# A fused attention and two-layer MLP kernel: third part of the values' product moved and widened, first loads on a second queue, schedule chosen anew

## The chip, the cores and the metric

The kernel runs on one core of one Trainium2 chip. The time is the device time of one execution in microseconds (us); the median of three runs of the kernel before is 1149.66 us (1148.32 to 1153.46). A profiled execution of the same kernel took 1149.11 us, and its trace spans 1147.1 us from the first to the last instruction.

## The reference

Attention over 4 batches and 8 heads, 576 tokens, head size 64, in which only scores within `tau` of a row's maximum count. Its output, as a 2304 x 512 matrix, goes through two MLP blocks with the weights' inner size 2048: the first with a squared ReLU, the second with a leaky ReLU.

```python
scores = scale * np.matmul(q, k.transpose(0, 1, 3, 2))
thresh = np.max(scores, axis=-1, keepdims=True) - tau
scores = np.where(scores >= thresh, scores, -1000000000.0)
attn = np.exp(scores - np.max(scores, axis=-1, keepdims=True))
attn = attn / (np.sum(attn, axis=-1, keepdims=True) + 1e-09)
attn_out = np.matmul(attn, v)
x = attn_out.transpose(0, 2, 1, 3).reshape(2304, 512)
h = x @ moe_w_in;  x = (np.maximum(h, 0) ** 2) @ moe_w_out
h = x @ moe2_w_in; x = np.maximum(0.01 * h, h) @ moe2_w_out
```

The weights arrive as 64-bit floats.

## The kernel before

**Attention.** Heads are taken in 16 pairs (`order`, four to a batch), and each pair in nine steps (`steps`): a step is 128 query rows of one head against all 576 keys, or, once in a pair, the last 64 rows of both heads. A step does its scores on PE (line 497), a row maximum on DVE (L507), the exponential on ACT (L508), threshold and sum on DVE (L512), and the normalization. In the first four pairs (`nav=4`) the normalized weights are turned on PE (L531) and multiplied with the values in fp32 (L597). From the fifth pair on they are split into a high and a low 16-bit part in one row `P16` of 1216 columns (576 high, the first 64 of them again, 576 low), turned by a DMA transpose (L559) and multiplied with the values by `av` (L593).

**The values' product (`values`).** For a chunk of 256 or 320 queries there are nine 128-row pieces of turned weights: four high, one that holds 64 high rows and 64 low rows, and four low. The values are split in a part `hi` that lies as 128 columns in `VA`, and a third part `low` of 64 columns in `VB`. A chunk is 15 matmuls: five with `hi` (128x128), four with `low` against the high pieces (64 columns, alternately in the lower and the upper half of the output), two with `low` against the mixed piece (its first 64 rows alone, half of the queries each), and four more with `hi` (128x128). There are 12 pairs with four chunks each, 48 chunks. ACT (L605, L607), POOL or DVE (L610) add the two halves of the output, and a DMA stores them in `x1d`.

**MLP.** `w_block` loads a block of raw weights (128 x 512 64-bit floats, 512 KB), turns them into fp32 in three DVE instructions (L341, L343, L345) and one on ACT (L340), and splits them into two fp32r parts (L285 or L287, then a subtraction on POOL or DVE, L296/L298). The raw blocks share a ring of three buffers (`wraw`). While attention runs, `ffn` takes 256 tokens at a time through 12 of the 16 blocks of the first layer (L641 and L665). After it the rest of the first layer and the second layer run in blocks of 512 tokens (L774 and L820), and the second layer's blocks of weights are prepared meanwhile.

**What sets the order.** Nothing is written out by hand: every operation is handed to `Plan.op` with its possible engines, a cost and a priority (an attention step number plus a constant of `CFG`). `Plan.order` simulates the engines with these costs, gives each operation to an engine (the multipliers `price` weigh the engines against each other), and issues all in the order of the simulated starts. So a changed constant can move operations in time and between engines anywhere. All loads and stores go through `dma` and are issued by SP; two small loads (`tau`, `eye`) are issued by ACT.

Of the kernel before, what the change touches and what calls it, by code (L numbers as in the profile page):

```python
# [18 lines left out]
P = 128  # L19
# [7 lines left out]
           {'V': 3.0, 'A': 0.99, 'G': 0.8},  # L27
           {'V': 2.4, 'A': 1.42, 'G': 1.25},
           {'V': 2.43, 'A': 1.06, 'G': 0.97},
           {'V': 3.0, 'A': 2.4, 'G': 1.02}],  # L30
    lead1=-2.0, xsg0=[0, 1, 2], lbm=8, lb=[[0, 2, 4, 6], [0], [2, 5], [1, 3, 5, 6]], xsm=4, xsg=[0, 3], dq=1.15,
    xu=False, pqk=-2.283, pd1=-0.75, pex=-1.0, pd2=0.3, ph=2.017, pl=1.4, hu=True, bg=2.008, lead=2.5, w0=22.0,
    wstep=2.3, fend=1.0, tol=0.2, hor=-0.015, xlead=5.801, nb=3, eb=3, pb=3, ptb=3, kvb=3, nat=(0, 1, 2, 3, 4, 5),
    nav=4, vb=2, tmb=1, gb=2, xb=1, w2step=2.0, wo=0.316, wrb=3, r1b=1, xrb=1,
# [211 lines left out]
def tile_kernel(ctx: ExitStack, tc: tile.TileContext, qT, kT, vv, w1, w2, tau, eye, out):  # L246
# [57 lines left out]
    def dma(o, i, r, w, prio, nbytes, **k):  # L304
        return op(("S", 0.06, lambda: nc.sync.dma_start(out=o(), in_=i())), r, w, prio, dma=move(nbytes), **k)
# [15 lines left out]
    def w_block(pool, src, f, tag, prio, after=()):  # L321
# [3 lines left out]
        for g, io in enumerate("io"):  # L325
# [4 lines left out]
            c = slice(g * W, (g + 1) * W)  # L330
            if wide:
# [7 lines left out]
                dma(lambda raw=raw: raw.get()[:, 0:2 * W].bitcast(I32), lambda c=c: src[f][:, c].bitcast(I32), [], [raw], pr - 1, P * W * 8, after=after)  # L339
# [69 lines left out]
    def prep(n):  # L409
# [9 lines left out]
        if n in CFG["nat"]:  # L419
# [6 lines left out]
            for h in range(2):  # L426
                dma(lambda h=h: qs(h)[h * D:(h + 1) * D], lambda h=h: qT[b, h0 + h], [], [Q], at(0), D * S * 4)
# [474 lines left out]
```

## Time and profile before

| | |
|---|---|
| runs, median (lowest to highest) | 1149.66 us (1148.32 to 1153.46) |
| profiled execution, its span | 1149.11 us, 1147.1 us |
| busy: PE, DVE, POOL, ACT | 94%, 60%, 55%, 47% of the span |
| mean granted TensorE clock | 0.990 of full speed |
| DMA | 121.82 MB, mean 106 GB/s |

An average over the span hides three stages. Up to about 125 us only attention runs; then attention and the MLP share PE until about 560 us; from there PE works almost without a gap to the end. The views by stretch show which engine is full in each, and the lists of waits show who is late.

### The profile page before, as it was taken

How to read it: one execution, taken by the hardware profiler on the slowest of the kernel's cores; microseconds unless marked ns; L12 is line 12 of the kernel's file. 1: busy time of each engine (PE TensorE's matmuls, PEld its weight loads, DVE VectorE, ACT ScalarE, POOL GpSimd, SP SyncE). 2: the span in 40 equal slices, each digit the busy share in tenths (PEclk: the TensorE clock that was granted, in tenths of full speed). 3: DMA queues.
4: the chain of work that ended last, by engine and by line, in shares of the span. 5: the costliest groups of instructions: out<-in, count | busy, mean ns of one | idle time of the engine just before them, and what ended most of it. 6: DMA issues, size and time to landing. Idle time of an engine off the chain costs nothing.

```text
span 1147.1 us, 17803 instructions
## 1 busy us (share of the span) xinstructions
PE 1076.0 (94%) x6308; PEld 885.2 (77%) x6308; DVE 691.4 (60%) x1293; ACT 533.9 (47%) x967; POOL 632.8 (55%) x653
## 2 busy tenths in 40 slices
PE   6878898998999899999899989999999999999998
PEld 3544587887878788888778768888888888888887
DVE  5999998788997678764869966381221221122122
ACT  5888778766777777664434432231111111121121
POOL 4677778778767777655756765562322232232222
PEclk9999999999999999999989999999999999999999
DMA  5444669888877777765543435540020010010010
GB/s 149 120 132 123 163 156 189 168 163 175 150 155 151 152 159 114 135 108 174 154 132 126 144 132 161 196 140 1 1 74 1 1 56 1 0 37 1 1 38 19
DMA packets 197672, 121.82 MB, mean 106 GB/s; under 512 B 156752, under 2 KB 175312, under 8 KB 197584
## 3 DMA queue, kind: packets, MB, share of 16 engines
q1 hardware_dynamic: 197296, 120.62, 44.6%
q8 instruction: 50, 0.82, 0.3%
q14 instruction: 38, 0.31, 0.1%
q10 hardware_dynamic: 288, 0.07, 0.0%
HBM read 70.98 MB, written 17.83 MB: 77 GB/s over the span
## 4 chain that ended last, share of the span: by engine, by line
PE 65%; DVE 11%; DMA 7%; issue 6%; ACT 6%; POOL 5%; SPq 1%; POOLq 0%; DVEq 0%; ACTq 0%
PE y L820 23%; PE h L774 22%; PE s L497 5%; PE o L593 5%; DMA PT<-P 4%; PE h L641 4%; PE y L665 3%; DVE wraw L343 2%; DVE e L512 2%; PE o L597 2%; DVE nb L507 2%; DVE wraw L345 1%; ACT e L508 1%; DVE P L553 1%; DVE wraw L341 1%
## 5 line engine op out<-in xcount | busy, mean ns | idle before, releaser
L298 POOL TENSOR_TENSOR gl<-r,gh 128x512 fp32r<-128x512 f32 (+1 forms) x150 | 194.9, 1300 | 311.1 <-DVE gh L287 269.4
L786 DVE TENSOR_TENSOR r<-h,r 128x512 f32<-128x512 f32 (+1 forms) x80 | 51.1, 638 | 287.7 <-ACT r L785 287.7
L785 ACT ACTIVATE r<-h 128x512 f32<-128x512 f32 (+1 forms) x80 | 44.4, 555 | 302.7 <-PE h L774 295.0
L497 PE MATMUL s<-KH,Q 128*128 128x288 f32 (+1 forms) x440 | 123.8, 376 | 18.1 <-DVE e L512 7.7
L507 DVE TENSOR_REDUCE nb<-s 128x1 f32<-128x576 f32 x144 | 107.6, 750 | 43.1 <-PE s L497 42.0
L512 DVE SCALAR_TENSOR_TENSOR e<-s,th,e 128x576 f32<-128x576 f32 x144 | 115.9, 809 | 15.5 <-ACT e L508 12.5
L508 ACT ACTIVATE e<-s,nb 128x576 f32<-128x576 f32 x144 | 106.0, 739 | 26.3 <-DVE nb L507 21.1
L497 PEld LDWEIGHTS s<-KH,Q 128*128 128x128 f32 (+1 forms) x440 | 75.4, 187 | 37.7 <-issue 22.4
L553 DVE SCALAR_TENSOR_TENSOR P<-e,r,P 128x576 f16<-128x576 f32 x77 | 85.1, 1107 | 5.2 <-ACT P L522 3.2
L343 DVE SCALAR_TENSOR_TENSOR wraw<-wraw 128x512 int32<-128x512 int32 x64 | 82.6, 1291 | 8.1 <-ACT wraw L340 4.4
L593 PE MATMUL o<-PT,VA 128*128 128x320 f16 (+1 forms) x432 | 70.7, 292 | 13.3 <-DMA PT<-P 10.5
L298 POOL TENSOR_TENSOR xl<-xr,xh 128x512 fp32r<-128x512 f32 (+1 forms) x52 | 67.9, 1313 | 26.4 <-ACT xh L285 24.2
L345 DVE SCALAR_TENSOR_TENSOR wraw<-wraw 128x512 int32<-128x512 int32 x64 | 66.5, 1040 | 1.0
L341 DVE TENSOR_SCALAR wraw<-wraw 128x512 int32<-128x512 int32 x64 | 51.3, 802 | 21.0 <-DMA wraw<-w 21.0
L285 ACT CAST gh<-r 128x512 fp32r<-128x512 f32 x66 | 40.8, 618 | 40.0 <-DVE r L783 28.7
L593 PEld LDWEIGHTS <-VA 128*128 128x128 bf16 x432 | 35.6, 99 | 28.9 <-DMA PT<-P 9.2
L497 PE MATMUL s<-KL,Q 128*128 128x288 f32 x200 | 56.3, 298 | 0.0
L510 POOL TENSOR_SCALAR th<-nb,ca 128x1 f32<-128x1 f32 x76 | 37.8, 497 | 26.3 <-DVE nb L507 19.6
L340 ACT ACTIVATE wraw<-wraw 128x512 f32<-128x512 f32 x64 | 43.3, 681 | 17.3 <-DMA wraw<-w 17.3
L522 ACT ACTIVATE P<-e,r 128x576 f16<-128x576 f32 x56 | 43.3, 774 | 16.5 <-DVE r L517 8.4
L605 ACT ACTIVATE tmp<-o 64x256 f32<-64x256 f32 (+1 forms) x64 | 26.1, 408 | 44.9 <-PE o L593 37.8
L298 POOL TENSOR_TENSOR P<-e,P 128x576 f16<-128x576 f32 x29 | 38.1, 1316 | 11.2 <-ACT P L285 6.4
(581 smaller groups left out, 3037.2 us busy)
## 6 DMA issues: line engine op xcount, KB each, us to landing
wraw<-w SPq DMA_DIRECT2D x64, 512.0 KB, 3.9
wraw<-qT SPq DMA_DIRECT2D x20, 288.0 KB, 4.1
wraw<-kT SPq DMA_DIRECT2D x20, 288.0 KB, 4.0
out<-yo SPq DMA_DIRECT2D x18, 256.0 KB, 2.0
VA<-vv SPq DMA_DIRECT2D x32, 128.0 KB, 3.0
x2d<-yo SPq DMA_DIRECT2D x16, 256.0 KB, 3.5
xr<-x2d SPq DMA_DIRECT2D x4, 1024.0 KB, 6.6
y1d<-ys SPq DMA_DIRECT2D x14, 256.0 KB, 2.7
```

The costliest lines, as they stand in the source:

```text
L298: alts.append(("G", pool2(n), lambda: nc.gpsimd.tensor_tensor(out=o(), in0=a(), in1=b(), op=alu), kind))
L341: op(("V", 0.7, lambda yi=yi: nc.vector.tensor_scalar(out=yi(), in0=yi(), scalar1=29, scalar2=None, op0=ALU.logical_shift_right)), [raw], ...
L343: op(("V", 0.9, lambda ui=ui, yi=yi: nc.vector.scalar_tensor_tensor(out=yi(), in0=ui(), scalar=3, in1=yi(), op0=ALU.logical_shift_left, op ...
L345: op(("V", 0.9, lambda ui=ui, yi=yi: nc.vector.scalar_tensor_tensor(out=yi(), in0=ui(), scalar=-(1 << 31), in1=yi(), op0=ALU.bitwise_and, ...
L497: nc.tensor.matmul(ps.get()[r, g, 0:S2], lhsT=o.Q.get()[:, q], rhs=(kk.get() if o.KL else f32(kk.get()))[:, g_(g)], start=k == 0 or not o. ...
L507: op(("V", 0.75, lambda: nc.vector.tensor_reduce(out=nb.get(), in_=pv(), axis=AX.XY, op=ALU.max, negate=True)), [ps], [nb], i + CFG["pd1"] ...
L508: op(("A", 0.76, lambda: nc.scalar.activation(e.get(), pv(), AF.Exp, bias=nb.get(), scale=1.0)), [ps, nb], [e], i + CFG["pex"], True)
L512: op(("V", 0.89, lambda: nc.vector.scalar_tensor_tensor(out=e.get(), in0=pv(), scalar=th.get(), in1=e.get(), op0=ALU.is_ge, op1=ALU.mult, ...
L553: op(("V", dve2(S), lambda: nc.vector.scalar_tensor_tensor(out=lo(), in0=ev(), scalar=r_.get(), in1=hi(), op0=ALU.mult, op1=ALU.subtract)) ...
L593: nc.tensor.matmul(ps.get()[r, c_], lhsT=f_(v)[0:rows], rhs=parts16(pt)[0:rows, j, c_], start=(k == 0), stop=(k == len(prods) - 1))
L774: nc.tensor.matmul(ps.get()[:, 0:n], lhsT=a.get()[:, kc * P:(kc + 1) * P], rhs=x.get()[:, kc, 0:n], start=(q == 0 and kc == 0), stop=(q == ...
L820: nc.tensor.matmul(o(), lhsT=l, rhs=r, start=(first and q == 0), stop=(last and q == 2))
```

## The change

Four things change. In `values` the four later `hi` matmuls now stand directly behind the first five, so that the nine 128x128 matmuls come first; the six with `low` come last, and the two on the mixed piece now take all 128 rows (its 64 low rows too) instead of 64. `dma` gets a parameter for the issuing engine, and ACT issues the two loads of the first pair's queries (`n` = 0) and the two loads of the first block of raw weights. These raw weights get a fixed priority of -2.8, ahead of the first pair's loads. And the constants in `CFG` differ, with the small change of the planner's costs for `av`.

```diff
     price=[{'V': 4.8, 'A': 1.81, 'G': 1.1},
-           {'V': 3.0, 'A': 0.99, 'G': 0.8},
+           {'V': 3.0, 'A': 0.84, 'G': 1.01},
...
-    xu=False, pqk=-2.283, pd1=-0.75, pex=-1.0, pd2=0.3, ph=2.017, pl=1.4, hu=True, bg=2.008, lead=2.5, w0=22.0,
+    xu=False, pqk=-2.996, pd1=-0.75, pex=-1.791, pd2=0.3, ph=2.017, pl=1.4, hu=False, bg=2.008, lead=2.5, w0=22.155,
...
-    def dma(o, i, r, w, prio, nbytes, **k):
-        return op(("S", 0.06, lambda: nc.sync.dma_start(out=o(), in_=i())), r, w, prio, dma=move(nbytes), **k)
+    def dma(o, i, r, w, prio, nbytes, q=nc.sync, **k):
+        return op(("S", 0.06, lambda: q.dma_start(out=o(), in_=i())), r, w, prio, dma=move(nbytes), **k)
...
+            first = pool == "wa" and src is w1 and f == 0
...
-                dma(lambda raw=raw: raw.get()[:, 0:2 * W].bitcast(I32), lambda c=c: src[f][:, c].bitcast(I32), [], [raw], pr - 1, P * W * 8, after=after)
+                dma(lambda raw=raw: raw.get()[:, 0:2 * W].bitcast(I32), lambda c=c: src[f][:, c].bitcast(I32), [], [raw], -2.8 if first else pr - 1, P * W * 8, after=after, q=nc.scalar if first else nc.sync)
...
-                dma(lambda h=h: qs(h)[h * D:(h + 1) * D], lambda h=h: qT[b, h0 + h], [], [Q], at(0), D * S * 4)
+                dma(lambda h=h: qs(h)[h * D:(h + 1) * D], lambda h=h: qT[b, h0 + h], [], [Q], at(0), D * S * 4, q=nc.sync if n else nc.scalar)
...
-        prods = [(slice(0, P), slice(0, w), P, j, hi, j) for j in range(NH)]
-        prods += [((lo3, up3)[j % 2], slice(0, w), P, j, low, j) for j in range(MAIN)]
-        prods += [(r, c_, REM, MAIN, low, MAIN) for r, c_ in ((lo3, slice(0, half)), (up3, slice(half, w)))]
-        prods += [(slice(0, P), slice(0, w), P, NH + j, hi, j) for j in range(MAIN)]
+        prods = [(slice(0, P), slice(0, w), j, hi, j) for j in range(NH)]
+        prods += [(slice(0, P), slice(0, w), NH + j, hi, j) for j in range(MAIN)]
+        prods += [((lo3, up3)[j % 2], slice(0, w), j, low, j) for j in range(MAIN)]
+        prods += [(r, c_, MAIN, low, MAIN) for r, c_ in ((lo3, slice(0, half)), (up3, slice(half, w)))]
...
-        for k, z, passes in () if n < CFG["nav"] else ((0, NH, NH), (NH, NH + MAIN + 2, 2.5), (NH + MAIN + 2, len(prods), MAIN)):
-            op(("T", passes * mm(w) + 0.15 * (k == NH), lambda k=k, z=z: av(k, z)), [pt, o.VA, o.VB], [ps], pr)
+        for k, z, passes in () if n < CFG["nav"] else ((0, NH, NH + 0.5), (NH, NH + MAIN, MAIN), (NH + MAIN, len(prods), 2.5)):
+            op(("T", passes * mm(w) + 0.2 * (k == NH + MAIN), lambda k=k, z=z: av(k, z)), [pt, o.VA, o.VB], [ps], pr)
```

Lines from the second hunk of the diff on stand one lower after the change (L341 becomes L342). The planner's order shows the change at three places.

On PE, inside one chunk of 320 queries of the values' product, before (`VA` is loaded for a product with `hi`, `VB` for one with `low`; the last numbers are output partitions x queries):

```order
L593 MATMUL o<-PT,VB 64x320
L593 LDWEIGHTS VB
L593 MATMUL o<-PT,VB 64x160
L593 LDWEIGHTS VB
L593 MATMUL o<-PT,VB 64x160
L593 LDWEIGHTS VA
L593 MATMUL o<-PT,VA 128x320
```

and the same place now, up to the instruction behind the chunk:

```order
L594 MATMUL o<-PT,VB 64x320
L594 LDWEIGHTS VB
L594 MATMUL o<-PT,VB 64x160
L594 LDWEIGHTS VB
L594 MATMUL o<-PT,VB 64x160
L642 MATMUL h<-xh,w5il 128x256 x4
```

The two narrow matmuls now end the chunk, and no product with `VA` follows them.

On ACT, the start of the program before:

```order
L309 DMA tau_sb<-tau 128x1
L689 DMA eye_sb<-eye 128x128
L508 ACT_TABLE_LOAD
L508 ACTIVATE e<-s,nb 128x576 x2
L400 ACTIVATE KH<-KH,qsc 128x576
```

and now, with the waits that the order shows:

```order
L309 DMA tau_sb<-tau 128x1
L305 DMA wraw<-w 128x1024
L305 DMA Q_118<-qT 64x576
L305 DMA wraw<-w 128x1024
L341 ACT_TABLE_LOAD
L341 ACTIVATE wraw<-wraw 128x512 [waits DMAHW2_49]
L305 DMA Q_118<-qT 64x576 [waits DMAHW5_49]
L690 DMA eye_sb<-eye 128x128 [waits DMAHW7_49]
L285 CAST w0ih<-wraw 128x512 [waits DVE_49]
L341 ACTIVATE wraw<-wraw 128x512
L509 ACTIVATE e<-s,nb 128x576 [waits DVE_49] x2
```

Two loads of raw weights stand ahead of and behind the first head's queries, and the second head's queries are issued behind an activation that waits for the first weights to land.

On DVE, the start of the program before:

```order
L316 TENSOR_SCALAR ca<-tau_sb 128x1
L507 TENSOR_REDUCE nb<-s 128x1 x2
L512 SCALAR_TENSOR_TENSOR e,sum<-s,th,e 128x576 x2
L517 RECIPROCAL r<-t 128x1
L507 TENSOR_REDUCE nb<-s 128x1
```

and now:

```order
L316 TENSOR_SCALAR ca<-tau_sb 128x1
L342 TENSOR_SCALAR wraw<-wraw 128x512
L344 SCALAR_TENSOR_TENSOR wraw<-wraw 128x512
L346 SCALAR_TENSOR_TENSOR wraw<-wraw 128x512
L342 TENSOR_SCALAR wraw<-wraw 128x512
L508 TENSOR_REDUCE nb<-s 128x1
L344 SCALAR_TENSOR_TENSOR wraw<-wraw 128x512
L508 TENSOR_REDUCE nb<-s 128x1
L513 SCALAR_TENSOR_TENSOR e,sum<-s,th,e 128x576
L346 SCALAR_TENSOR_TENSOR wraw<-wraw 128x512
L513 SCALAR_TENSOR_TENSOR e,sum<-s,th,e 128x576
```

Six conversions of raw weights, which stood behind the first six attention steps' work or among it, now stand ahead of the first maximum (four of them) and between the first steps (two).

## Rows read from the trace of the kernel before

**Rows 1.** The page, busy time of each engine over the span.
```profile
PE 1076.0 (94%) x6308; PEld 885.2 (77%) x6308; DVE 691.4 (60%) x1293; ACT 533.9 (47%) x967; POOL 632.8 (55%) x653
```
**Rows 2.** Busy time by stretch: length, us and instructions of each, clock, DMA, GB/s.
```profile
0.00:12.00 12.00, 4.18 (x8) 2.52 (x8) 2.03 (x6) 2.14 (x3) 4.17 (x12) 1.00 0.91 193
12.00:124.00 112.00, 91.69 (x504) 55.93 (x506) 104.50 (x221) 92.05 (x159) 80.16 (x123) 1.00 0.44 129
124.00:500.00 376.00, 349.24 (x2743) 303.79 (x2741) 313.40 (x680) 279.47 (x521) 279.27 (x307) 0.99 0.81 154
575.00:582.00 7.00, 6.45 (x16) 5.06 (x17) 6.90 (x9) 4.17 (x7) 3.84 (x3) 0.52 0.87 265
582.00:720.00 138.00, 133.52 (x569) 107.63 (x568) 104.75 (x124) 49.98 (x87) 82.23 (x60) 0.99 0.44 138
720.00:1147.00 427.00, 423.14 (x1963) 348.12 (x1961) 109.95 (x199) 71.76 (x131) 135.28 (x114) 1.00 0.11 36
```
**Rows 3.** Waits of PE over the span: total us, times, longest.
```profile
PE o L593 <- DMA PT<-P: 10.5, 14, 2.0
...
PE h L774 <- DVE r L783: 3.7, 1, 3.7
```
**Rows 4.** Waits of DVE from 124 to 500 us.
```profile
DVE nb L507 <- PE s L497: 31.2, 39, 2.4
```
**Rows 5.** Timeline, DVE at the start: start, duration, instruction, [idle before, releaser].
```profile
9.18 0.76 DVE L507 TENSOR_REDUCE nb<-s 128x1 f32<-128x576 f32 x1 [4.27 <-PE s L497]
11.10 0.76 DVE L507 TENSOR_REDUCE nb<-s 128x1 f32<-128x576 f32 x1 [1.16 <-PE s L497]
```
**Rows 6.** Timeline, SP's issue of the first queries.
```profile
1.66 0.57 SPq L305 DMA_DIRECT2D Q<-qT  x1
```
**Rows 7.** Timeline, PE's first matmul of the first head, then of the second head.
```profile
6.88 0.82 PE L497 MATMUL s<-KH,Q 128*128 128x288 f32 x1 [6.88 <-DMA Q<-qT]
...
12.69 0.48 PE L497 MATMUL s<-KH,Q 128*128 128x288 f32 x1 [1.63 <-issue]
```
**Rows 8.** DMA from 0 to 6.88 us, then from 0 to 12 us.
```profile
DMA packets 1726, 1.16 MB, mean 169 GB/s; under 512 B 1234, under 2 KB 1362, under 8 KB 1726
...
DMA packets 3483, 2.32 MB, mean 193 GB/s; under 512 B 2670, under 2 KB 2798, under 8 KB 3483
```
**Rows 9.** Groups by line, DVE from 12 to 124 us: busy us, mean ns.
```profile
L343 DVE SCALAR_TENSOR_TENSOR wraw<-wraw 128x512 int32<-128x512 int32 x16 | 17.8, 1110 | 0.1
L341 DVE TENSOR_SCALAR wraw<-wraw 128x512 int32<-128x512 int32 x17 | 14.5, 850 | 0.0
L345 DVE SCALAR_TENSOR_TENSOR wraw<-wraw 128x512 int32<-128x512 int32 x16 | 13.4, 837 | 0.0
```
**Rows 10.** Timeline, PE, one chunk of 320 queries.
```profile
197.09 0.85 PE L593 MATMUL o<-PT,VA 128*128 128x320 f16 x5 [0.26 <-DMA PT<-P]
197.87 0.65 PE L593 MATMUL o<-PT,VB 128*64 128x320 f16 x6
198.46 0.72 PE L593 MATMUL o<-PT,VA 128*128 128x320 f16 x4
```
**Rows 11.** Timeline, weight loads of the same chunk.
```profile
197.87 0.14 PEld L593 LDWEIGHTS <-VB 128*64 128x64 bf16 x4 [0.26 <-issue]
198.26 0.11 PEld L593 LDWEIGHTS <-VB 64*64 64x64 bf16 x2 [0.25 <-issue]
```
**Rows 12.** Line 593: a matmul's ns, min/median/max; idle time before the line, us and times.
```profile
L593 PE MATMUL o<-PT,VA x432: 269/298/437, 130.2 to 518.8; 128*128 128x256 f16 x72, 128*128 128x320 f16 x72
...
  issue: 30.4, 108
```
**Rows 13.** Timeline, DVE ahead of the first MLP unit behind attention.
```profile
569.02 1.62 DVE L343 SCALAR_TENSOR_TENSOR wraw<-wraw 128x512 int32<-128x512 int32 x1
...
572.78 0.42 DVE L341 TENSOR_SCALAR wraw<-wraw 128x512 int32<-128x512 int32 x1
```
**Rows 14.** Groups by line, DVE from 0 to 560 us: a subtraction of one 128x512 tile.
```profile
L296 DVE TENSOR_TENSOR gl<-r,gh 128x512 fp32r<-128x512 f32 x4 | 4.4, 1106 | 0.4 <-ACT gh L285 0.3
```

More of the change, by code (lines that the diff above doesn't have):

```diff
@@ L26 @@
     price=[{'V': 4.8, 'A': 1.81, 'G': 1.1},
[L27 to L34 removed]
+           {'V': 3.0, 'A': 0.84, 'G': 1.01},
+           {'V': 2.82, 'A': 1.42, 'G': 1.25},
+           {'V': 1.99, 'A': 1.06, 'G': 1.2},
+           {'V': 3.0, 'A': 2.4, 'G': 1.5}],
+    lead1=-2.0, xsg0=[0, 1, 2, 3], lbm=8, lb=[[0, 4], [0], [5], [0, 1, 2, 3, 5, 6]], xsm=4, xsg=[0, 3], dq=1.15,
+    xu=False, pqk=-2.996, pd1=-0.75, pex=-1.791, pd2=0.3, ph=2.017, pl=1.4, hu=False, bg=2.008, lead=2.5, w0=22.155,
+    wstep=2.3, fend=1.0, tol=0.2, hor=-0.021, xlead=5.801, nb=3, eb=3, pb=3, ptb=3, kvb=3, nat=(0, 1, 2, 3, 4, 5),
+    nav=4, vb=2, tmb=1, gb=2, xb=1, w2step=2.57, wo=0.316, wrb=3, r1b=1, xrb=1,
 )
@@ L584, in values @@
         hi, low = (lambda j: o.up()[:, j, h].rearrange("p a d -> p (a d)")), (lambda j: o.VB.get()[:, j, h])
-        prods = [(slice(0, P), slice(0, w), P, j, hi, j) for j in range(NH)]
-        prods += [((lo3, up3)[j % 2], slice(0, w), P, j, low, j) for j in range(MAIN)]
-        prods += [(r, c_, REM, MAIN, low, MAIN) for r, c_ in ((lo3, slice(0, half)), (up3, slice(half, w)))]
-        prods += [(slice(0, P), slice(0, w), P, NH + j, hi, j) for j in range(MAIN)]
+        prods = [(slice(0, P), slice(0, w), j, hi, j) for j in range(NH)]
+        prods += [(slice(0, P), slice(0, w), NH + j, hi, j) for j in range(MAIN)]
+        prods += [((lo3, up3)[j % 2], slice(0, w), j, low, j) for j in range(MAIN)]
+        prods += [(r, c_, MAIN, low, MAIN) for r, c_ in ((lo3, slice(0, half)), (up3, slice(half, w)))]
         def av(k0, k1):
             for k in range(k0, k1):
-                r, c_, rows, j, f_, v = prods[k]
-                nc.tensor.matmul(ps.get()[r, c_], lhsT=f_(v)[0:rows], rhs=parts16(pt)[0:rows, j, c_], start=(k == 0), stop=(k == len(prods) - 1))
+                r, c_, j, f_, v = prods[k]
+                nc.tensor.matmul(ps.get()[r, c_], lhsT=f_(v), rhs=parts16(pt)[:, j, c_], start=(k == 0), stop=k >= len(prods) - 2)
         def av32():
```

## The prediction

> **What bounds the kernel now.** I read the page's busy line first: PE is busy for 94% of the span, no other engine for more than 60% [rows 1]. That is a mean over stages, so the second view is busy time by stretch [rows 2]. From 720 us to the end PE is busy for 423.14 of 427 us: nothing there can be won except by taking matmul work away, and the change takes none away there. From 124 to 500 us PE is busy for 349.24 of 376 us (93%), DVE for 313.40 (83%). From 12 to 124 us the order is the other way round: DVE 104.50 of 112 us (93%), PE 91.69. So DVE's work sets the pace up to about 124 us, and PE's behind it. The lists of waits bear this out: between 124 and 500 us DVE waits 31.2 us for scores from PE [rows 4], while PE's longest wait of the whole span is 10.5 us for turned weights [rows 3]. Last, I read the timelines of the two places that the code change touches, the start [rows 5 to 8] and one chunk of the values' product [rows 10, 11], and of the way from attention into the MLP [rows 13].
>
> **The values' product.** In a chunk PE loads weights of three shapes: 128*128, then 128*64, then 64*64, then 128*128 again. Ahead of the 128*64 and of the 64*64 load it idles 0.26 and 0.25 us [rows 11]. What this costs is read from the starts of the matmuls. Five of 320 queries take 0.85 us; the last one starts one duration before its end, and with 0.30 us for one [rows 12] four distances are 0.55 us, so 0.137 us each [rows 10]. The six with the third part are 4/2 + 2 x 1/4 = 2.5 such distances, because two that write different halves of the output run side by side: 0.344 us. From the first of them to the next 128*128 matmul 198.46 - 197.87 = 0.59 us pass [rows 10]. So 0.245 us are lost in two changes of shape, 0.12 each. The change lets the two narrow matmuls take 128 rows, so they have the shape of the four ahead of them: one change of shape is gone. Putting them last does not remove another, since the instruction behind a chunk is of shape 128*128 nearly always: before there were 128 to 64 columns, to 64*64, back; now there are 128 to 64 columns, back. The 64 rows more I count at nothing, since the four matmuls ahead of them, with 128 rows, fit the same price for each query; were the pair to take twice its 0.07 us, it would be 48 x 0.07 = 3.3 us.
>
> 48 chunks x 0.12 = 5.8 us of PE. Bounds: nothing, if PE waits behind the chunk anyway, and 30.4 / 108 x 48 = 13.5 us by the idle time that the profile puts ahead of such loads [rows 12], which counts time in which the last matmuls still run. I take 0.12, from starts, and 93% of the sum, PE's share of busy time in this stretch: **-5.4 us**.
>
> **The start.** Before, the first head's queries are SP's third load, issued at 1.66 us [rows 6], landing at 6.88 us, when 1.16 MB had moved [rows 7, 8]; the first maximum starts at 9.18 us, and DVE idles 4.27 us ahead of it and 1.16 us ahead of the second [rows 5]. Now ACT issues tau, 512 KB of raw weights, the first queries (144 KB), and 512 KB again. DVE has four conversions ahead of the first maximum: 0.850 + 1.110 + 0.837 + 0.850 = 3.65 us at their mean price up to 124 us, and a fifth of 1.110 us fits the gap of 1.16 us ahead of the second maximum [rows 5, 9]. The sixth stands where DVE is busy and gains nothing. So 4.76 us of DVE work move from a stretch in which DVE is 93% busy into time in which it idles: 4.4 us.
>
> Against it stands that the fourth conversion, and behind it the first maximum, waits for the second block of raw weights. 1168 KB stand in ACT's queue up to its end, and SP can have issued 848 KB beside it (two loads of keys, one of values, one of queries: 288, 128, 288 and 144 KB). 2.02 MB had moved before at 6.88 + (2.02 - 1.16) / 0.227 = 10.6 us, by the 1.16 MB between 6.88 and 12 us [rows 8]. With 0.42 us for the conversion alone on its port [rows 13] the first maximum starts at 11.0 instead of 9.18 us: 1.8 us late. Bounds: not later at all, if the 1168 KB go first (1.16 MB had landed at 6.88 us), and 12.4 us (3.2 late), if both queues carry the same amount (2.32 MB at 12 us, rows 8). What queues behind the waiting instructions: on DVE the maximum, on ACT the second head's queries, which are issued only when the first weights and the first queries have landed. They are not needed before the second pair of score buffers is free, at 12.69 us before [rows 7], so they are just in time. Sum of the start: 1.8 - 4.4 = **-2.6 us**, between -5.2 (no delay, all six conversions hidden) and -0.2 (3.65 us hidden, 3.2 late).
>
> The Trainium skill bears on this: its page "DMA: Bandwidth & Descriptors", in "Issuing engines are not separate DMA queues" and "Rules for kernel authors", says that loads issued by SP and ACT run on the same 16 DMA engines and interleave, so that a second issuing engine saves issue time and gives no bandwidth. By that rule the second queue is no gain for the queries, and what moves ahead of them delays them; it is the upper bound of the delay just worked out, and stands as a rival below. No run so far shows two full queues side by side.
>
> **The schedule.** The order moves work from POOL to DVE and ACT: DVE goes from 1151 to 1174 instructions, ACT from 971 to 986, POOL from 656 to 628. Most of it is subtractions of one tile, 1.1 us each on DVE [rows 14]. From 575 us on DVE has room: 33 us of 138 idle between 582 and 720 us, and 317 of 427 behind [rows 2]; that is worth nothing. In the attention part the additions and removals, by the order's counts and each group's mean, leave DVE with an estimated 4 us more, within the 62.6 us in which it idles between 124 and 500 us [rows 2]. One place matters: ahead of the first MLP unit behind attention PE waits 3.7 us for DVE [rows 3], and then runs 7 us at a granted clock of 0.52, the lower of its two levels, 1.2 GHz [rows 2], which costs half of the time, 3.4 us. By the order, DVE has one raw block less ahead of that unit (four instructions, 1.62 + 1.66 + 0.43 + 0.42 = 4.1 us; the first and the last are shown, rows 13) and four subtractions more (4 x 1.1 = 4.4 us): no difference. I take **0** for the schedule; bounds are -7.1 (the wait and the slow stretch both go) and +4.1 (one block more ahead of the unit). How far the 26.8 us in which PE idles between 124 and 500 us move is not to be read from before; the engines' sums do not change enough to move them one way.
>
> **Sum.** 1149.11 - 5.4 - 2.6 = 1141.1 us for an execution like the profiled one. That one lies 0.55 us below the median of the runs shown, so I forecast **1141.7 us**; its own range is 1137 to 1146.
>
> **Rivals.**
> - *The way into the MLP opens.* Fewer subtractions on POOL free the raw buffers sooner, the 3.7 us wait goes, and with it the stretch at half clock: 1141.7 - 7.1 = 1134.6 us. For it speaks that the three raw buffers are released by POOL, against it that DVE's sum ahead of the unit is the same.
> - *The gains are eaten.* The start's delay is at its upper bound (-0.2), and the 5.4 us turn into waits for DVE or POOL, because these don't get faster with PE: 1149.66 - 0.2, at most 1 or 2 us less, 1148 us. Against it stand the 31.2 us in which DVE waits for PE [rows 4]. That the narrow matmuls' change of shape is already hidden belongs here too.
> - *Both queues share evenly.* The first maximum starts 3.2 us late instead of 1.8: 1143.1 us. For it speaks that the DMA engines are 91% busy up to 12 us [rows 2]. This is what that rule of the Trainium skill gives.
> - *Slower: turned weights come later.* Normalizing is no longer marked urgent (`hu`), so DVE, ACT and POOL may take other work ahead of it, and the transposes are issued later; PE then waits in more chunks. Now it waits in 14 chunks for 10.5 us, 0.75 each [rows 3]; if the other 34 wait as long, it is 25.5 us more: 1167 us. From 19 chunks more it is slower than 1155.4. Against it stands that the product with the values is ordered by the same estimate as the transposes.
>
> **How the numbers follow.** About 0.5% (5.75 us) is what a measurement of this kernel can tell from no change: faster means below 1143.9, slower above 1155.4. The forecast has a chance of 0.40 (0.33 of it faster, 0.07 within), even queues 0.12 (0.07 and 0.05), the opened way 0.17 (all faster), eaten gains 0.20 (0.01 and 0.19), late transposes 0.11 (0.10 slower, 0.01 within). Faster 0.58, same 0.32, slower 0.10. The range from 1132 to 1150.5 holds the forecast, the even queues and most of the opened way and the eaten gains.
>
> **What would show it.** In the profile after, a chunk has no load of shape 64*64; idle time ahead of line 594 occurs some 60 times instead of 108; from the first product of a chunk to the instruction behind it pass 0.12 us less. The first maximum on DVE starts near 11 us, and six conversions stand ahead of 15 us. The first MLP matmul (L642) starts some 2.6 us earlier than at present, the first long run of L775 some 8. I am wrong if the first maximum starts behind 13 us, if PE waits for turned weights in 30 chunks or more, or if DVE's idle time between 124 and 500 us shrinks below 30 us.

## The result, and the profile after

The changed kernel takes 1132.97 us (median of 4 runs, 1129.32 to 1137.38), the kernel before 1149.88 us beside it: ratio 0.985 [0.9808, 0.9893], 16.9 us faster. The forecast was 1141.7 us, 8 us faster, with a range from 1132 to 1150.5. So the sign was right, the time lies 1 us inside the lower end of the range, and the sizes of all three terms were wrong: of the 5.4 us that I took for the values' product between nothing and 3 came, the start lost where I had a gain, and the schedule, which I took at 0, gave all that is left.

The profiled execution took 1133.95 us (span 1132.2). Its busy line, as in [rows 1]:

```profile
PE 1070.7 (95%) x6308; PEld 883.8 (78%) x6308; DVE 689.3 (61%) x1316; ACT 544.4 (48%) x978; POOL 596.4 (53%) x626
```

PE is busy 5.3 us less than before, the span is 14.9 us shorter, so PE idles 9.6 us less. POOL has lost 36.4 us of work and 27 instructions, ACT has taken 10.5 us. Busy time by stretch (length; us and instructions of PE, PEld, DVE, ACT, POOL; PE clock; DMA share; GB/s), as in [rows 2]:

```profile
0.00:12.00 12.00, 1.56 (x3) 1.18 (x4) 2.18 (x6) 1.97 (x2) 3.12 (x9) 1.00 0.83 216
12.00:124.00 112.00, 92.46 (x476) 56.09 (x474) 92.13 (x220) 86.36 (x150) 73.87 (x108) 1.00 0.43 119
124.00:500.00 376.00, 354.01 (x2818) 310.72 (x2818) 315.52 (x697) 296.25 (x544) 280.67 (x324) 1.00 0.82 158
575.00:582.00 7.00, 7.00 (x32) 5.64 (x31) 4.84 (x7) 1.24 (x2) 1.53 (x1) 1.00 0.57 166
```

The reader is to see two opposite things. Up to 12 us PE has 1.56 us of work instead of 4.18: the start is late. From 124 to 500 us PE gets 354.01 us of work done instead of 349.24, at a clock of 1.00 instead of 0.99: the middle is denser. The waits of PE over the span (us, times, longest), as in [rows 3]:

```profile
PE o L594 <- DMA PT<-P: 10.8, 10, 2.7
PE s L498 <- DMA Q<-qT: 10.4, 1, 10.4
...
PE h L775 <- DVE r L784: 1.8, 1, 1.8
```

The first line is as before (10.5 us), the second is the late start (6.88 us before [rows 7]), the third was 3.7 us. DVE's wait for scores from 124 to 500 us, as in [rows 4], went from 31.2 to 25.9 us.

The start itself, in the timeline (start, duration, instruction, idle time before it and its releaser), answers to [rows 5 to 7]:

```profile
1.17 0.46 ACTq L305 DMA_DIRECT2D wraw<-w  x1
...
1.67 0.53 ACTq L305 DMA_DIRECT2D Q<-qT  x1
...
2.23 0.59 ACTq L305 DMA_DIRECT2D wraw<-w  x1
...
7.54 0.43 DVE L342 TENSOR_SCALAR wraw<-wraw 128x512 int32<-128x512 int32 x1 [2.08 <-DMA wraw<-w]
...
10.33 0.47 ACTq L305 DMA_DIRECT2D Q<-qT  x1
10.44 4.18 PE L498 MATMUL s<-KH,Q 128*128 128x288 f32 x8 [10.44 <-DMA Q<-qT]
...
12.52 0.43 DVE L342 TENSOR_SCALAR wraw<-wraw 128x512 int32<-128x512 int32 x1 [2.84 <-DMA wraw<-w]
12.86 0.75 DVE L508 TENSOR_REDUCE nb<-s 128x1 f32<-128x576 f32 x1
```

The queries, issued at 1.67 us as before, land at 10.44 us instead of 6.88. The second block of raw weights lands only at 12.52 us, and the first maximum stands behind it at 12.86. The DMA engines moved 2.59 MB up to 12 us, against 2.32 [rows 8]:

```profile
DMA packets 2682, 2.59 MB, mean 216 GB/s; under 512 B 1937, under 2 KB 1937, under 8 KB 2682
```

The late start is paid a second time, in PE's clock. PE's second group of eight scores, of the second head, before and now:

```profile
12.69 2.23 PE L497 MATMUL s<-KH,Q 128*128 128x288 f32 x8 [1.63 <-issue]
...
16.98 4.18 PE L498 MATMUL s<-KH,Q 128*128 128x288 f32 x8 [2.35 <-DVE e L513]
```

One of these matmuls, in the changed kernel up to 26.3 us, and in s2 (the changed kernel with one number moved, see below) from 121 to 130 us, where the granted clock on record is 0.53 (ns, lowest/median/highest):

```profile
L498 PE MATMUL s<-KH,Q x21: 554/687/820, 10.4 to 26.1; 128*128 128x288 f32 x21
...
L498 PE MATMUL s<-KH,Q x8: 687/687/849, 121.1 to 128.5; 128*128 128x288 f32 x8
```

From 27 to 60 us the median is 406 ns. So PE ran at the lower level, 1.2 GHz, up to some 26 us. The records of the clock begin with its first rise, at 11.7 us before and at 26.4 us now; the 1.00 that the views show ahead of it isn't measured. Up to the first matmul of the MLP PE is busy for 102.26 us now and was for 97.78 before, with the same 520 matmuls.

To compare many kernels I cut each span in three: up to the first MLP matmul (L641 before, L642 after), the middle up to the first `y` matmul of the MLP behind attention (L820, L821), and the rest. "Waits" is the sum of PE's waits in the middle, in brackets those for POOL and for DVE. "Half" is the time at the lower clock of 1.2 GHz (the clock's own records, which begin with its first rise, without the last 25 us). All of it is from the one profiled execution of each, the median and ratio from all runs.

| kernel | median | ratio | up to MLP | middle | waits (POOL, DVE) | rest | half |
|---|---|---|---|---|---|---|---|
| before | 1149.9 | 1 | 125.9 | 454.9 | 34.2 (6.0, 11.2) | 566.3 | 20.4 |
| after | 1133.0 | 0.985 | 133.7 | 435.2 | 22.8 (0, 5.3) | 563.3 | 6.8 |
| e1 product alone | 1148.3 | 0.9989 | 125.6 | 454.6 | 36.1 (5.3, 11.1) | 566.3 | 20.4 |
| e2 after, old product | 1131.6 | 0.9847 | 129.5 | 436.0 | 22.1 (0, 6.3) | 562.7 | 3.4 |
| e3 after, one queue | 1129.1 | 0.9811 | 125.8 | 437.5 | 23.5 (0, 6.8) | 563.2 | 10.2 |
| e4 after, no early loads | 1141.0 | 0.9929 | 134.1 | 439.9 | 27.2 (0, 7.3) | 563.1 | 27.3 |
| e6 table alone | 1146.6 | 0.998 | 133.7 | 445.2 | 28.4 (1.4, 15.2) | 565.7 | 30.6 |
| e5 early loads alone | 1169.5 | 1.0166 | 127.6 | 479.1 | 49.1 (2.8, 21.3) | 563.5 | 61.3 |
| e7 after, old table | 1158.7 | 1.0081 | 128.5 | 460.2 | 41.2 (8.4, 11.4) | 563.8 | 30.6 |
| s1 before, shaken | 1151.1 | 1.0026 | 125.4 | 458.6 | 38.9 (1.8, 18.0) | 563.4 | 27.2 |
| s2 after, shaken | 1133.2 | 0.9841 | 136.3 | 434.7 | 23.8 (0, 7.7) | 562.7 | 17.0 |

Between the first two rows: up to the MLP +7.8 us, the middle -19.7, the rest -3.0, together -14.9, the difference of the spans. Of the middle's 19.7 us, 11.4 are waits (34.2 to 22.8), and the stretches at half clock in it went from 17.0 to 6.8 us, worth at most half of that, 5.1 us. 3 us or a little more stay for the product and what the order brings forward. The 7.8 us up to the MLP are, nearly, the 3.7 us by which the first maximum is late and the 4.5 us that PE is busy longer. In e4 and e6 one chunk of the values' product and twelve score matmuls more stand ahead of the first MLP matmul (547 matmuls instead of 520), in e5 and e7 four scores fewer, so their first two columns can't quite be set against the others.

### The profile page after: what moved, and what is told of

Its sections match the earlier page's. It is cut to its first block, busy times and chain, and to the rows that moved or that the text cites. A ratio compares the mean times of both kernels' runs of the same rounds, so it can differ in the third digit from the quotient of the medians.

```text
span 1132.2 us, 17792 instructions
## 1 busy us (share of the span) xinstructions
PE 1070.7 (95%) x6308; PEld 883.8 (78%) x6308; DVE 689.3 (61%) x1316; ACT 544.4 (48%) x978; POOL 596.4 (53%) x626
## 4 chain that ended last, share of the span: by engine, by line
PE 71%; DVE 6%; DMA 5%; issue 3%; ACT 3%; POOL 2%; SPq 0%; POOLq 0%; DVEq 0%; ACTq 0%
PE y L821 23%; PE h L775 22%; PE y L666 8%; PE h L642 7%; PE o L594 5%; PE s L498 5%; DMA PT<-P 4%; DVE wraw L344 2%; DVE wraw L346 1%; ACT e L509 1%; DVE e L513 1%; DVE nb L508 1%; DVE wraw L342 1%; POOL gl L298 0%; PE o L598 0%
## 5 line engine op out<-in xcount | busy, mean ns | idle before, releaser
L298 POOL TENSOR_TENSOR gl<-r,gh 128x512 fp32r<-128x512 f32 (+1 forms) x140 | 182.0, 1301 | 323.6 <-DVE gh L287 272.8
L498 PE MATMUL s<-KH,Q 128*128 128x288 f32 (+1 forms) x440 | 125.9, 381 | 16.6 <-DMA Q<-qT 10.4
L508 DVE TENSOR_REDUCE nb<-s 128x1 f32<-128x576 f32 x144 | 107.9, 750 | 39.7 <-PE s L498 38.9
L498 PEld LDWEIGHTS s<-KH,Q 128*128 128x128 f32 (+1 forms) x440 | 76.8, 190 | 37.5 <-issue 18.3
L298 POOL TENSOR_TENSOR xl<-xr,xh 128x512 fp32r<-128x512 f32 (+1 forms) x49 | 65.6, 1347 | 30.4 <-ACT xh L285 24.3
L594 PE MATMUL o<-PT,VA 128*128 128x320 f16 (+1 forms) x432 | 63.3, 290 | 13.8 <-DMA PT<-P 10.8
L344 DVE SCALAR_TENSOR_TENSOR wraw<-wraw 128x512 int32<-128x512 int32 x64 | 68.5, 1070 | 8.5 <-ACT wraw L341 5.2
L346 DVE SCALAR_TENSOR_TENSOR wraw<-wraw 128x512 int32<-128x512 int32 x64 | 62.1, 970 | 1.1
L594 PEld LDWEIGHTS <-VA 128*128 128x128 bf16 x432 | 38.8, 99 | 28.7 <-issue 10.9
L285 ACT CAST gh<-r 128x512 fp32r<-128x512 f32 x67 | 41.2, 616 | 32.0 <-DVE r L784 22.6
L523 ACT ACTIVATE P<-e,r 128x576 f16<-128x576 f32 x60 | 46.2, 772 | 20.4 <-DVE r L518 8.9
L498 PE MATMUL s<-KL,Q 128*128 128x288 f32 x200 | 55.7, 294 | 0.0
L341 ACT ACTIVATE wraw<-wraw 128x512 f32<-128x512 f32 x64 | 43.7, 683 | 20.9 <-DMA wraw<-w 20.4
L342 DVE TENSOR_SCALAR wraw<-wraw 128x512 int32<-128x512 int32 x64 | 43.5, 683 | 13.6 <-DMA wraw<-w 13.6
L511 POOL TENSOR_SCALAR th<-nb,ca 128x1 f32<-128x1 f32 x73 | 31.3, 429 | 31.1 <-DVE nb L508 16.3
L609 POOL TENSOR_TENSOR xs<-xs,tmp 64x256 f32<-64x256 f32 (+1 forms) x40 | 36.0, 901 | 19.4 <-ACT xs L608 16.5
L287 DVE CAST gh<-r 128x512 fp32r<-128x512 f32 (+1 forms) x87 | 37.9, 437 | 8.7 <-PE y L821 0.6
```

The costliest lines, as they stand in the source:

```text
L298: alts.append(("G", pool2(n), lambda: nc.gpsimd.tensor_tensor(out=o(), in0=a(), in1=b(), op=alu), kind))
L344: op(("V", 0.9, lambda ui=ui, yi=yi: nc.vector.scalar_tensor_tensor(out=yi(), in0=ui(), scalar=3, in1=yi(), op0=ALU.logical_shift_left, op ...
L498: nc.tensor.matmul(ps.get()[r, g, 0:S2], lhsT=o.Q.get()[:, q], rhs=(kk.get() if o.KL else f32(kk.get()))[:, g_(g)], start=k == 0 or not o. ...
L508: op(("V", 0.75, lambda: nc.vector.tensor_reduce(out=nb.get(), in_=pv(), axis=AX.XY, op=ALU.max, negate=True)), [ps], [nb], i + CFG["pd1"] ...
L594: nc.tensor.matmul(ps.get()[r, c_], lhsT=f_(v), rhs=parts16(pt)[:, j, c_], start=(k == 0), stop=k >= len(prods) - 2)
```

## The experiments

**The product: e1 and e2.** Theory A: a chunk saves only the 0.04 us by which the instruction behind it comes earlier after the change, 2 us in all. Theory B, the prediction: the 0.12 us of each chunk are real, and the product alone gives 5.4 us. e1 is the kernel before with the new order of matmuls and the 128 rows, e2 the changed kernel with the old one; the order of everything else is kept as it was.

```diff
+        prods = [(slice(0, P), slice(0, w), j, hi, j) for j in range(NH)]
+        prods += [(slice(0, P), slice(0, w), NH + j, hi, j) for j in range(MAIN)]
+        prods += [((lo3, up3)[j % 2], slice(0, w), j, low, j) for j in range(MAIN)]
...
```

> The kernel before, with the new order and the 128 rows of the values' product alone; the planner keeps its old costs, so every engine's order is that of before except inside a chunk. Theory A (the new product saves what its matmul starts show after the change, 0.03 to 0.05 us a chunk, and the schedule did the rest): 48 x 0.04 = 2 us, 1148 us. Theory B (the prediction: a change of shape less saves 0.12 us a chunk): 5.4 us, 1144.5 us.

> The changed kernel, with the old order and the 64 rows of the values' product; the planner keeps the new costs, so every engine's order is that of the changed kernel except inside a chunk. Theory A: 2 us slower than the changed kernel, 1135 us. Theory B: 5.4 us slower, 1138.4 us.

e1: 1148.25 us against 1148.69, ratio 0.9989 [0.9974, 1.0005]; e2: 1131.64 us, 0.9847 [0.9825, 0.987], no slower than the changed kernel. The product is worth between nothing and 3 us: theory B falls. The same chunk of 320 queries as in [rows 10] in e1, PE's timeline:

```profile
195.71 1.40 PE L593 MATMUL o<-PT,VA 128*128 128x320 f16 x9
197.04 0.53 PE L593 MATMUL o<-PT,VB 128*64 128x320 f16 x6
197.50 0.39 PE L665 MATMUL y<-gh,w11oh 128*128 128x256 f32 x1
```

From the chunk's start to the start of the same MLP matmul behind it pass 197.50 - 195.71 = 1.79 us; before, the chunk started at 197.09 [rows 10] and that matmul at 198.90, 1.81 us:

```profile
198.90 0.39 PE L665 MATMUL y<-gh,w11oh 128*128 128x256 f32 x1
```

Over all chunks with no idle time behind them the medians are 1.79 against 1.81 us with 320 queries and 1.48 against 1.53 us with 256. Yet the idle time ahead of weight loads of line 593 fell from 30.4 us in 108 places [rows 12] to

```profile
  issue: 22.9, 59
```

The row has lost nearly half its places, and the kernel at most 3 us of its time. Where the 0.12 us went, the starts tell. The way in costs the same: nine distances of 0.137 us are 1.233 us, and the first narrow matmul starts at 1.33; before, five are 0.685 us, and it started at 0.78. From the first narrow matmul to the next wide one 0.46 us pass instead of 0.59, and the six are worth 0.344: so 0.12 us are lost there instead of 0.245, just as forecast. But in the old chunk four wide matmuls follow, and from the first of them to the instruction behind the chunk 198.90 - 198.46 = 0.44 us pass, not four distances, 0.55: there 0.11 us of the loss are made up. In the new chunk nothing stands behind the narrow ones that could make up for it. Why the instruction behind the wide ones starts so early isn't shown.

**The start: e3, e8, e9, e10.** e3 keeps the order of the changed kernel and lets SP issue these loads too. e8 keeps two queues, with the queries ahead of the weights on ACT's; e9 also puts the second block of weights behind the first two sums on DVE. e10 does what e9 does on one queue.

```diff
-                dma(... -2.8 if first else pr - 1, P * W * 8, after=after, q=nc.scalar if first else nc.sync)
+                dma(... -2.8 if first else pr - 1, P * W * 8, after=after, q=nc.sync)
...
-                dma(... at(0), D * S * 4, q=nc.sync if n else nc.scalar)
+                dma(... at(0), D * S * 4, q=nc.sync)
```

> The changed kernel in the same order on every compute engine, with the first queries and weights issued by SP instead of ACT (SP: keys, weights, first head's queries, weights, second head's queries). If the second queue itself is worth the 8 us that the kernel without it lost, this one is near 1141 us. If that loss came from the plan made anew (its low-clock stretches), the queue is worth next to nothing: 1131 to 1134 us, with the second head's scores earlier, since its queries no longer wait behind an activation.

1129.1 us (1123.38 to 1133.01), 0.9811 [0.9786, 0.9835]. The second queue gains nothing; by the medians it costs 4 us, though the intervals of e3 and of the changed kernel overlap. Here the start is not late. Its timeline:

```profile
1.19 0.42 SPq L305 DMA_DIRECT2D wraw<-w  x1
1.66 0.56 SPq L305 DMA_DIRECT2D Q<-qT  x1
2.26 0.57 SPq L305 DMA_DIRECT2D wraw<-w  x1
...
6.23 0.43 DVE L342 TENSOR_SCALAR wraw<-wraw 128x512 int32<-128x512 int32 x1 [1.28 <-DMA wraw<-w]
...
7.46 3.78 PE L498 MATMUL s<-KH,Q 128*128 128x288 f32 x8 [7.46 <-DMA Q<-qT]
...
8.88 0.43 DVE L342 TENSOR_SCALAR wraw<-wraw 128x512 int32<-128x512 int32 x1 [0.50 <-DMA wraw<-w]
...
9.75 0.76 DVE L508 TENSOR_REDUCE nb<-s 128x1 f32<-128x576 f32 x1 [0.44 <-PE s L498]
```

The same loads in the same order, queries between the two blocks of weights: the queries land at 7.46 us instead of 10.44, the blocks at 6.23 and 8.88 instead of 7.54 and 12.52. Not all of it is the queue: in e2, with the same loads on two queues as the changed kernel, the first scores start at 9.05 us and the second block's conversion at 10.73. Both versions move 216 GB/s up to 12 us, so the second queue brought no bandwidth; it mixed later loads of SP into what is needed first (up to 12.5 us ACT's queue carried 1.20 MB of the 2.72 that the changed kernel moved). What the Trainium skill says in "DMA: Bandwidth & Descriptors" ("Issuing engines are not separate DMA queues"), that loads of several issuing engines interleave on the same 16 DMA engines, agrees with this pair.

> The changed kernel in the same order, except that ACT issues both heads' queries ahead of the two loads of weights. The first scores start near 7 us instead of 10.4 and the second head's near 14 instead of 17, but DVE still has the conversion that waits for the second weights ahead of the first maximum, so that stays near 12.5 us: 1 to 2 us faster than the changed kernel, 1131.5 us. If the late queries are what costs the start, the first maximum comes near 9.5 us and the gain is 3 us or more.

> As the kernel with the queries first, and the second block of weights is converted behind the first two steps' sums instead of ahead of and between them. If waiting for the second weights is what holds the first maximum, it starts near 10 us, and the first stage ends about 3 us earlier than in the changed kernel: 1130 us. If the start's delay is absorbed later anyway, no change: 1133 us.

e8: 1134.7 us, 0.9872 [0.9843, 0.9901]; e9: 1131.61 us, 0.9839 [0.9821, 0.9856]. Neither can be told from the changed kernel. In both the queries land near 7.2 us, and still the first maximum comes at 12.9 us. In e9 (L502 is there what L498 is in the changed kernel, L344 is L342, and L512 is L508):

```profile
7.30 4.18 PE L502 MATMUL s<-KH,Q 128*128 128x288 f32 x8 [7.30 <-DMA Q<-qT]
...
10.81 0.43 DVE L344 TENSOR_SCALAR wraw<-wraw 128x512 int32<-128x512 int32 x1 [4.70 <-DMA wraw<-w]
...
12.87 1.42 DVE L512 TENSOR_REDUCE nb<-s 128x1 f32<-128x576 f32 x2
```

The first block's conversion still stands ahead of it in DVE's order, and that block now lands at 10.81 us instead of 7.54. DVE idles 4.70 us for it, and the maximum waits behind it: a load that is moved off one wait shows up in the next.

> The changed kernel with all loads issued by SP, the first queries ahead of the two early blocks of raw weights, and on DVE the second block behind the first two sums. If the delay of the start on two queues is what stands between the changed kernel and its best: first maximum at 9.0 to 9.8 us (12.9 in the changed kernel), first MLP matmul near 126 us instead of 133.7, and 1124 to 1130 us, at or below the 1129.1 us of the version with one queue. If the early conversions of the second block were worth their place ahead of the first maximum, or the middle takes back what the start gains (as with two queues, where the queries first gave nothing): 1130 to 1134 us.

1130.26 us (1127.01 to 1134.13), 0.9831 [0.9788, 0.9874]: it can't be told from e3. First maxima at 10.23 us, first MLP matmul at 130.5 instead of the 126 expected, so the second expectation holds: the first conversion waits 3.3 us for its block in front of the maxima, and from 12.7 to 19.5 us the granted clock is 0.50. By the medians no version of the start beats e3's, with the queries between the blocks on one queue; the intervals of e3, e9 and e10 overlap.

**The schedule: e4, e6, e5, e7.** Three parts are left: the table of numbers (`CFG`), the early loads (raw weights at priority -2.8, second queue), and the product's costs in the planner. e4 is the changed kernel without the early loads and the second queue, e6 the kernel before with the new table, e5 the kernel before with the early loads, e7 the changed kernel with the old table. Each is planned anew.

```diff
-           {'V': 3.0, 'A': 0.84, 'G': 1.01},
+           {'V': 3.0, 'A': 0.99, 'G': 0.8},
...
-    xu=False, pqk=-2.996, pd1=-0.75, pex=-1.791, pd2=0.3, ph=2.017, pl=1.4, hu=False, bg=2.008, lead=2.5, w0=22.155,
+    xu=False, pqk=-2.283, pd1=-0.75, pex=-1.0, pd2=0.3, ph=2.017, pl=1.4, hu=True, bg=2.008, lead=2.5, w0=22.0,
```

(The edit of e7; e6 is the same lines the other way round in the kernel before.)

> The changed kernel without the second queue: SP issues the first queries and weights again, and the first weights have their old priority (planned anew with the new constants). Theory A (the second queue and the early weights made the start later, by 3 to 4 us at the thirtieth step): the first maximum starts near 9.2 us again and the time is 3 us below the changed kernel, 1130 us. Theory B (the prediction: the start gains 2.6 us): 1135.6 us.

> The kernel before with the new constants alone (old product, one queue, planned anew). Theory A (the schedule is worth most of the change): 14 us or more off before, 1136 us or less. Theory B (the product and the start are worth 8 us, the schedule the other 9): 1141 us.

> The kernel before (old product, old table of numbers) with only the loads changed: first queries and the first two blocks of raw weights on ACT's queue, the weights' loads at the priority -2.8; the order of all else is planned anew with the old table. Theory A (the middle gains because the first weights are converted in the idle start and DVE, POOL and ACT have that work behind them afterwards): first maximum near 12.9 us, the stretch from the first MLP matmul to the first long run of y some 440 us or less instead of 455, and 1133 to 1139 us. Theory B (the table of numbers is what shortens the middle, the early weights only move the start): first MLP matmul some 5 us later, the middle 450 us or more, and 1147 to 1153 us. Theory C (both are needed, one without the other keeps the stretches of half clock or the idle time): between, 1140 to 1146 us.

> The changed kernel with the old table of numbers: new product, second queue, early weights, planned anew with the old table. Theory A (early weights): 1133 to 1138 us, PE idle in the middle stretch under 27 us (34.6 before, 23.3 after). Theory B (the table of numbers): 1146 to 1152 us, PE idle in the middle over 32 us, since the product alone gave about 1 us and the early weights only delay the start. Theory C (both are needed): 1140 to 1145 us.

Measured: e4 1140.98 us, 0.9929 [0.9904, 0.9955]; e6 1146.6 us, 0.998 [0.996, 1.0]; e5 1169.51 us, 1.0166 [1.0119, 1.0212]; e7 1158.71 us, 1.0081 [1.0057, 1.0106]. e4 and e6 lie above both of their expectations, and none of the three for e5 and e7 had them slower than the kernel before by 21 and 10 us: theory A (early weights alone) falls, theory B (the table) is too kind to them, and C is right only in that both are needed. The table is worth 2 us with the old code and 1158.7 - 1133.0 = 25.7 us with the new. The early loads cost 10 us (e7 against e1) or 21 (e5) with the old table, and with the new one they are worth 8 (e4 against after). e2 does without the new product and e3 without the second queue (the planner's costs for the product are the new ones in both), and neither loses anything. So no part carries the gain: the table and the early loads do it together. I call that the fit of the table to the code.

What fits, the waits of PE show. In the middle of e5, the kernel with the early loads and the old table:

```profile
PE o L594 <- DMA PT<-P: 16.7, 13, 2.9
PE s L498 <- DVE e L513: 9.8, 9, 4.1
PE h L775 <- DVE r L784: 5.9, 1, 5.9
PE s L498 <- DVE th L510: 3.1, 1, 3.1
```

and in the middle of e7, where only the product and its costs in the planner differ besides:

```profile
PE o L594 <- DMA PT<-P: 8.2, 9, 2.8
PE h L775 <- DVE r L784: 5.7, 1, 5.7
PE y L666 <- POOL gl L298: 5.6, 3, 2.2
PE h L642 <- ACT xh L285: 4.9, 2, 4.4
...
PE h L642 <- POOL xl L298: 2.8, 2, 2.0
```

In the changed kernel's middle the same view reads, between the wait for turned weights and the one at L775 (10.8 and 1.8 us, both shown above):

```profile
PE h L642 <- ACT r L649: 2.6, 4, 1.0
PE s L498 <- DVE e L513: 2.2, 4, 1.2
```

The wait for turned weights (`PT<-P`) that led the list before still leads it. What went are waits for POOL and DVE, 1 to 6 us each. The new table charges POOL more (`G` 0.8 to 1.01, 0.97 to 1.2, 1.02 to 1.5), and every kernel with it has POOL busy for 592 to 606 us instead of 631 to 640, and waits for POOL in the middle of 0 to 1.4 us; with the old one they are 1.8 to 8.4. It does not do it alone: e6 has traded them for waits for DVE (15.2 us). e4, with the new product besides, has both short (0 and 7.3 us) and still loses, mostly to the clock: its span is 10.6 us longer than that of e3, the like of it with the early loads, and 17.1 us more of it are at half clock, worth up to 8.5 us. Part of the fit may be that DVE is less busy up to 124 us (92.13 us instead of 104.50 [rows 2]), and this not because fewer weights are converted: the groups of the changed kernel from 0 to 124 us (busy us, mean ns), against [rows 9],

```profile
L344 DVE SCALAR_TENSOR_TENSOR wraw<-wraw 128x512 int32<-128x512 int32 x16 | 16.0, 1002 | 0.8 <-ACT wraw L341 0.8
L346 DVE SCALAR_TENSOR_TENSOR wraw<-wraw 128x512 int32<-128x512 int32 x16 | 11.7, 734 | 0.1
L342 DVE TENSOR_SCALAR wraw<-wraw 128x512 int32<-128x512 int32 x16 | 8.6, 543 | 4.9 <-DMA wraw<-w 4.9
```

are 48 instructions instead of 49 and take 36.3 us instead of 45.7, each group with a shorter mean. But e5, the slowest kernel, has the lighter DVE too (92.82 us from 12 to 124 us), so this can't be enough. That the prices of POOL and the lighter DVE are the reason for the fit is my reading of these rows; no run changes the prices of POOL alone.

A long wait of PE is paid twice. In e5, busy time by 5 us (columns as above):

```profile
285.00:290.00 5.00, 1.30 (x4) 0.98 (x4) 2.94 (x8) 1.95 (x6) 1.05 (x2) 0.60 0.97 196
290.00:295.00 5.00, 4.05 (x20) 2.65 (x21) 4.25 (x10) 2.44 (x4) 3.16 (x6) 0.50 0.96 204
295.00:300.00 5.00, 3.48 (x16) 3.18 (x16) 3.62 (x9) 3.68 (x9) 3.54 (x3) 0.50 0.24 39
300.00:305.00 5.00, 5.00 (x31) 4.78 (x31) 4.58 (x8) 2.90 (x6) 2.63 (x5) 0.69 1.05 150
```

From 285 to 290 us PE stands idle for 3.7 of 5 us; there the granted clock falls, and from 290 to 300 us it is 0.50, the lower level of 1.2 GHz, to come back in the last row: 17.1 us in all. PE is busy for 11.9 of them, and half of that, some 6 us, is the cost on top of the idle time. In the changed kernel only one such place is left between 140 and 560 us, and it is short:

```profile
195.00:200.00 5.00, 2.09 (x15) 1.89 (x15) 4.93 (x12) 3.78 (x7) 2.70 (x5) 1.00 0.95 179
200.00:205.00 5.00, 4.21 (x22) 2.52 (x23) 2.05 (x6) 2.12 (x4) 3.54 (x3) 0.66 1.08 183
```

**Luck of the order: s1 and s2.** One number of the table is moved by a little in each kernel, so that the order changes for no reason, at several hundred places in s1 and some hundred in s2.

```diff
-    ... lead=2.5, w0=22.0,
+    ... lead=2.5, w0=22.05,
...
-    ... hor=-0.021, xlead=5.801, ...
+    ... hor=-0.021, xlead=5.75, ...
```

> The kernel before with one number of its table moved by a little (due time of the weights 22.05 instead of 22.0), which changes several hundred places of its order for no reason. If any new order of this kernel lies within some 2 us, 1147 to 1151 us, and the 15 us of the change are more than a draw from the orders. If the time before was an unlucky draw: 1143 us or less, and part of the change's gain is luck. The half-clock stretches are then fewer than 20 us.

> The changed kernel with one constant moved by 1% (xlead 5.801 to 5.75), which has no aim: the planner moves some hundred rows. If the schedule's gain lies in the placement of single instructions (who is late at a dozen places, and whether PE's clock falls behind it), the time moves by several us, most likely up: 1133 to 1142 us, with more low-clock stretches. If it lies in the engines' shares and priorities, it stays within 1.5 us of the changed kernel, 1131.5 to 1134.5 us.

s1: 1151.13 us, 1.0026 [1.0002, 1.0051]; s2: 1133.18 us, 0.9841 [0.981, 0.9871]. Both stay with their kernel within 3 us, so neither time hangs on one exact order; s1 had 27.2 us at half clock, not fewer than 20 as the second expectation wanted, and s2 reached the time of the changed kernel with 17.0 instead of 6.8. One small move each is no more than that. e5 and e7 differ only in the product and its costs in the planner and lie 10.8 us apart, of which e1 gives the product 3 at most: about 8 us can come from planning anew alone (61.3 us at half clock against 30.6). How much of the 16.9 us is a fit of the table, and how much a good draw among the orders that it can give, these runs don't settle.

## Why the prediction was right in sign and wrong in its terms

**What bounds the kernel.** Behind 124 us this held: the dense rest moved only from 566.3 to 563.3 us. "So DVE's work sets the pace up to about 124 us" did not: up to its first MLP matmul DVE is busy for 101.39 us in e3 instead of 108.41, and that matmul starts at 125.8 us as before (125.9). What does set the pace there, these runs don't show.

**The values' product, -5.4 us forecast.** The mechanism was named rightly (a chunk has no 64*64 load, idle places fell to 60 as forecast), and its price was wrong: from the start of a chunk to the next instruction 0.02 us (320 queries) and 0.05 (256) were saved instead of 0.12. Over 48 chunks that is 1.8 us, and e1 measured 0.4 (between 3.0 less and 0.6 more). The step that failed: "So 0.245 us are lost in two changes of shape, 0.12 each. [...] one change of shape is gone." The 0.12 us are indeed gone up to the next wide matmul, but I took what is lost up to there as lost for good. In the old chunk the four wide matmuls behind it made up 0.11 us by the instruction behind the chunk, the only start that counts. The low bound ("nothing") was the right end. That the pair with all 128 rows costs nothing fits the rows: from it to the instruction behind pass 0.17 us, before 0.19.

**The start, -2.6 us forecast.** The first maximum came at 12.86 us, not 11.0, a little behind the 12.4 of my outer bound, and the first MLP matmul 7.8 us later instead of 2.6 earlier. The step that failed: "1168 KB stand in ACT's queue up to its end, and SP can have issued 848 KB beside it". When the second block landed, at 12.52 us, not 2.02 MB had moved but more than the 2.59 of the first 12 us: ACT's queue had carried 1.20 MB of 2.72 by then, which was the rival *both queues share evenly*, and the trace is on that side. (The 2.02 MB are 2016 KB of 1024 bytes, so 2.06 by the view's measure, which would make 0.2 us.) Its price of 3.2 us was near the 3.7 by which the first maximum came late, but it left out what follows. The second head's scores started at 16.98 instead of 12.69 us, 4.3 later. It was not their queries, issued at 10.33 us, that held them (in e8 these are issued by 2.4 us, and the scores start at 16.77), but DVE's first sum, behind the late maxima. And PE, idle for 2.35 us between the two heads, stayed at 1.2 GHz up to 26 us, which I had at nothing. The 4.4 us that I had freed DVE of did not show as an earlier MLP: e3, whose maxima come on time, starts it at 125.8 us, where before started it (125.9). The delay varies, and these two parts make it up: in e2, with the same order of loads, the first maximum is 2.2 us late, PE is busy for 2.0 us more up to the MLP, and that starts 3.6 us late (129.5); in the changed kernel it is 3.7, 4.5 and 7.8, in e8 3.7, 1.8 and 5.3.

**The schedule, 0 forecast.** This is where the gain is: 19.7 us in the middle. The step that failed: "How far the 26.8 us in which PE idles between 124 and 500 us move is not to be read from before; the engines' sums do not change enough to move them one way". The sums of DVE did stay (60.5 us idle between 124 and 500 us, against the 62.6 of before), and PE's idle time moved all the same, from 26.8 to 22.0 us there and from 34.2 to 22.8 us of waits in the whole middle, because, as I read the waits, it hangs on which single instruction is late, not on a sum. My bounds, -7.1 to +4.1, priced one place, the way into the MLP, which did open: the wait went from 3.7 to 1.8 us and the half clock behind it from 6.8 to 3.4 us, so about 3.6 us of the 7.1, and the first matmul of L775 came 7.0 us earlier (8 forecast), the first `y` 11.9. They left out the other waits for POOL and DVE and the half clock behind them.

**The rivals.** *The way opens* came at half its price. *Late transposes* did not: waits for turned weights stayed at 10.8 us in 10 chunks, well below the 30 that I had named as fatal. *Gains are eaten* was right on the product and wrong on the total. The three slips against each other (5, 10 and -20 us) left the total just inside the range, which is luck as much as bounds.

## What to carry to other kernels

An idle row ahead of a weight load is not a price: compare start to start across the whole group, up to the next instruction behind it, before a change of shape is charged. A second issuing engine moved no more bytes here; put first what is needed first, on one queue, and look where each load lands, and up to when PE's matmuls take their time at the lower clock. A planner's table belongs to the code that it was fitted to: change the code and fit again before judging the edit, since the early loads cost 10 to 21 us with the old numbers and were worth 8 with the new; and plan anew more than once, since one order is one draw.

## What was not expected of the hardware

The same conversions on DVE took 543 instead of 850 ns (L342), 734 instead of 837 (L346), when the order around them had changed; what beside them slows them is not settled here. With two queues a 144 KB load issued at the same time let PE start at 10.44 us (9.05 in e2) instead of 7.46, although both versions moved 216 GB/s. PE stayed at 1.2 GHz up to 26.4 us after a start 3.6 us later, and up to 11.7 us before. In the middle a wait of PE of 1.8 us (ahead of L775 in the changed kernel) was followed by 3.4 us at half clock, and one of 4.1 us in e5 by 17.1, so that of the difference in the middle between before and after up to a quarter is clock (5.1 of 19.7 us).
